# Fetching v behind a tile's second value products, identity products in the opening, and new ranks in a planned attention and feed-forward kernel

## The chip, the cores and the metric

The kernel runs on one core of a Trainium2 chip. The metric is the device time of the whole program in microseconds. Before the change it was 361.08 us, the median of three runs that went from 360.38 to 366.06. The engines are called as the profile calls them: PE is TensorE (PEld its weight loads), DVE is VectorE, ACT is ScalarE, POOL is GpSimd and SP is SyncE, which only issues transfers here.

## The reference

The program is an attention with a window of 32 positions and 8 global positions, followed by a feed-forward layer with softplus.

```python
batch, n_heads, seq, head_dim = (8, 8, 576, 64)
...
scores = scale * np.matmul(q, k.transpose(0, 1, 3, 2))
mask = np.abs(pos[:, None] - pos[None, :]) <= window
mask = mask | is_global[:, None] | is_global[None, :]
scores = np.where(mask, scores, -1000000000.0)
attn = softmax(scores)
x = np.matmul(attn, v)                    # to (8 * 576, 512)
h = x @ w_in                              # 512 -> 2048
g = np.maximum(h, 0.0) + np.log1p(np.exp(-np.abs(h)))
out = g @ w_out                           # 2048 -> 512
```

The softmax is written as one call here. Inputs and output are float32; the kernel computes products in bfloat16.

## The kernel before

**Units and tiles.** The 4608 tokens are cut into 72 units of 64 (9 to a batch). Four units make a quarter tile `n4` (18 of them), and two of these a tile `m` of 512 tokens (9 tiles, numbered 0 to 8 here). A batch boundary falls inside a tile as a rule.

**Preparing a batch.** `load_main` and `load_rest` (L260, L264) fetch k and q into `nq`; TensorE transposes them (`tk`, L614; in batch 0 `tk` L592 and `tq` L603), and the copies go to `kx` and `qx`. `pick` (L537, L548) takes the global rows out, `turn` (L559, tile `gt`) transposes them. `sg` (L677) makes the scores of the global rows, `ov` (L720) their output, which ends in `oz`.

**A unit.** `sc` (L770) makes the scores `s`; `top` (L776, DVE) adds the mask and finds the largest; `ex` (L809, ACT) makes the exponentials `pe`; `su` (L817 to L819, DVE) the sums and `rs`; `no` (L825, POOL) the normalised `pn`, and `gc` (L829, POOL) the columns of the global keys. `pn` is transposed to `pt`. For the first 16 units, and some at the end, TensorE does it (`tp`, L835) and ACT or DVE copies the result. For the others SP issues a DMA transpose (L847).

**Value products.** `val` makes the output `xo` of four units: products with `oz` (L893) and with v in `vA` and `vB` (L906). It needs `pt` of its four units. `xev` copies `xo` to `xT`. `vA` holds a batch's v in 128-row blocks, `vB` the same shifted by 64 rows: SP copies it from `vA` (`shift`, L514 and L515). Both have two buffers, so batch b's v is written over batch b-2's. Five fetches on POOL's queue bring it (`load_v`, L275).

**The feed-forward layer.** `first` (L949) makes `h` in 16 chunks of four matmuls, `soft` (L955, ACT) the softplus `g`; `second` (L960) makes `o` in 4 groups of 16 matmuls, `oev` copies it to `osb`, and SP writes that out (L967). In tile 0 the 512 columns of `h` are cut in two halves. The order of a stage is so: during a tile's `o`, the units of the next tile go through `ex` to `pt`; both its `val` follow, the second one at the very end, and then the next tile's `h` begins.

**The planner.** None of this is in the order in which it is written. Every piece of work is a job with an engine (or two to choose from), a cost, a rank and dependencies. `_Order.run` (L87) takes, again and again, the job that can start soonest by its own costs, the lowest rank first among equals. It gives out PSUM banks by kind (`KINDS`: how many a kind may hold, how many are left spare) and doubles TensorE's costs until some time after the job marked `warms`. The program is then emitted in that order, engine by engine, and each engine works its list in order. The ranks are given at each `o.add` and corrected by three tables: `OPENING`, `LATER` and `OWN`.

Two more things set the fetch of v. The loads of batch b wait for `val` of the quarter tiles that hold units of batch b-2 (L1138), and the loads of k and q of batch b+1 wait for the last fetch of v of batch b (L1086).

```python
    for b in range(2, B):
        held = [T["val", n4] for n4 in range(NU) if any((n4 * 4 + u) // NJ == b - 2 for u in range(4))]
        for job in T["load", b, 2]:
            job["deps"] += [*held, T["ov", b - 2], T["shift", b - 2]]
```

## Time and profile before

| what | value |
|---|---|
| median of three runs | 361.08 us |
| the profiled execution | 360.17 us |
| its span, first to last instruction | 358.3 us |
| mean granted TensorE clock | 0.990 |
| PE, DVE, ACT, POOL busy | 332.8, 224.9, 265.6, 158.4 us |
| first matmul | 6.57 us |
| h of tile 0 begins | 31.01 us |
| h of tiles 1 to 4 begins | 75.15, 115.95, 153.38, 189.68 us |
| transposes by DMA (48), median from issue to landing | 3.6 us |
| fetches of v (40), 96 or 128 KB each, median to landing | 6.4 and 6.8 us |

A busy time is the time in which an engine had an instruction in hand. A row of the view in order of time merges neighbours of one kind: it gives the start of the first, the time until the end of the last, the count, and in brackets the idle time of the engine before it with what ended that. A matmul's end is modelled and reaches some 0.17 us past the start of the next one, so distances are best taken from start to start. "SPq" is the issue of a transfer on SP's queue, not the transfer.

### The profile page before, as it was taken

Reading aid. Unit: us, or ns where it says so; the run is one execution under the profiler, and the core shown is the slowest. Engines: PE = TensorE matmul, PEld = TensorE weight load, DVE = VectorE, ACT = ScalarE, POOL = GpSimd, SP = SyncE. Lnnn points to the kernel's source line nnn. Section 1 sums busy time; section 2 is a strip of 40 time slices with the busy share of each in tenths; the row PEclk is TensorE's granted clock in tenths of the full one; section 3 lists DMA queues with packets and bytes.
Section 4 is the critical chain, followed back from the end, with each engine's and each line's share of the span. In section 5 each row is a group of like instructions: output and inputs, shape, how many; then the busy total and the mean of one; then the engine's idle time right before and its main releaser. Section 6 shows DMA issues by size and latency. Waiting matters only on the chain.

```text
span 358.3 us, 11513 instructions
## 1 busy us (share of the span) xinstructions
PE 332.8 (93%) x4382; PEld 176.5 (49%) x4434; DVE 224.9 (63%) x1044; ACT 265.6 (74%) x738; POOL 158.4 (44%) x268
## 2 busy tenths in 40 slices
PE   1989989999996999999989999999899999999996
PEld 1546775554454444554445445544454454454444
DVE  5886468977696566966796468666865783072011
ACT  3699669985895659885987698859875986774610
POOL 7989732880097204950495047604830370060000
PEclk9999999999997899999999999999999999999999
DMA  6999996099259922997399827993992222021002
GB/s 93 144 235 198 201 133 126 31 153 221 52 129 119 195 44 77 146 159 135 83 132 159 143 82 119 152 166 88 119 118 60 63 82 55 0 75 60 1 29 88
DMA packets 94007, 40.01 MB, mean 112 GB/s; under 512 B 76800, under 2 KB 87424, under 8 KB 93952
## 3 DMA queue, kind: packets, MB, share of 16 engines
q0 software_dynamic: 57056, 18.36, 57.7%
q1 hardware_dynamic: 36896, 20.92, 25.2%
q8 instruction: 34, 0.56, 0.7%
q14 instruction: 21, 0.17, 0.2%
HBM read 36.71 MB, written 9.44 MB: 129 GB/s over the span
## 4 chain that ended last, share of the span: by engine, by line
PE 70%; DMA 8%; DVE 8%; ACT 6%; issue 4%; POOL 3%; SPq 0%; POOLq 0%; DVEq 0%; ACTq 0%
PE h L949 36%; PE o L960 20%; DMA pt<-pn 7%; DVE sm L817 3%; PE s L770 3%; PE xo L906 2%; ACT pe L809 2%; POOL pn L825 2%; DMA kn<-in_k_dram 2%; PE tk L614 1%; PE tp L835 1%; DVE rs L819 1%; ACT L690 1%; ACT pg L690 1%; DVE osb L491 1%
## 5 line engine op out<-in xcount | busy, mean ns | idle before, releaser
L825 POOL TENSOR_TENSOR pn<-pe,rs 128x512 bf16<-128x512 f32 x72 | 74.9, 1041 | 152.5 <-DVE rs L819 140.4
L949 PE MATMUL h<-xT,win 128*128 128x512 bf16 (+1 forms) x620 | 132.7, 362 | 1.3 <-issue 0.2
L960 PE MATMUL o<-wout,g 128*128 128x512 bf16 (+1 forms) x560 | 128.0, 373 | 3.3 <-issue 2.5
L955 ACT ACTIVATE g<-h 128x512 bf16<-128x512 f32 (+1 forms) x160 | 85.2, 557 | 44.7 <-PE h L949 44.3
L809 ACT ACTIVATE pe<-st,nb 128x136 f32<-128x136 f32 x288 | 93.0, 403 | 0.9 <-DVE nb L776 0.9
L949 PEld LDWEIGHTS <-win 128*128 128x128 bf16 x640 | 60.7, 99 | 61.0 <-issue 4.8
L776 DVE CUSTOM_DVE_ANT_0 st<-s,mask 128x136 f32<-128x136 f32 x288 | 65.9, 295 | 38.2 <-PE s L770 38.2
L960 PEld LDWEIGHTS <-g 128*128 128x128 bf16 x592 | 55.1, 98 | 57.0
L817 DVE TENSOR_REDUCE sm<-pe 128x4 f32<-128x544 f32 x60 | 42.6, 710 | 10.7 <-ACT pe L809 10.7
L275 POOL DMA_DIRECT2D vA<-in_v_dram x40 | 34.2, 864 | 0.0
L491 DVE COPY osb<-o 128x512 f32<-128x512 f32 (+1 forms) x23 | 15.3, 664 | 27.5 <-PE o L960 27.2
L776 DVE DVE_READ_ACCUMULATOR2_ANT nb<- 128x1 f32 x288 | 24.0, 83 | 0.0
L819 DVE TENSOR_TENSOR rs<-rs,notg 128x4 f32<-128x4 f32 x72 | 17.9, 249 | 2.5
L491 DVE CAST xT<-xo 128x512 bf16<-128x512 f32 x20 | 13.6, 686 | 7.6 <-PE xo L906 7.5
L491 ACT COPY kx<-tk 128x32 bf16<-128x32 bf16 (+2 forms) x85 | 17.5, 310 | 0.9 <-PE tq L614 0.5
L491 ACT CAST xT<-xo 128x512 bf16<-128x512 f32 x16 | 9.4, 586 | 11.6 <-PE xo L906 11.5
L829 POOL TENSOR_TENSOR gw<-pe,rs 128x32 bf16<-128x32 f32 x72 | 17.2, 240 | 1.0 <-ACT R L491 0.5
L818 DVE RECIPROCAL rs<-sm 128x4 f32<-128x4 f32 x72 | 12.8, 177 | 7.7 <-ACT pe L809 1.5
L770 PE MATMUL s<-kx,qx 64*64 64x136 bf16 x576 | 15.3, 235 | 1.9 <-PE h L949 1.0
L491 DVE COPY qx<-tq 128x512 bf16<-128x512 bf16 (+3 forms) x43 | 16.3, 430 | 1.0 <-PE tq L614 0.7
L906 PE MATMUL xo<-pt,vB 128*64 128x64 bf16 x256 | 12.9, 203 | 3.9 <-DMA pt<-pn 3.9
L770 PEld LDWEIGHTS <-qx 64*64 64x64 bf16 x576 | 10.0, 111 | 12.6 <-issue 12.3
(125 smaller groups left out, 327.1 us busy)
## 6 DMA issues: line engine op xcount, KB each, us to landing
out_dram<-osb SPq DMA_DIRECT2D x35, 256.0 KB, 2.2
vB<-vA SPq DMA_DIRECT2D x16, 256.0 KB, 7.3
nq<-in_k_dram POOLq DMA_DIRECT2D x7, 512.0 KB, 8.1
nq<-in_q_dram POOLq DMA_DIRECT2D x7, 512.0 KB, 12.4
vA<-in_v_dram POOLq DMA_DIRECT2D x24, 128.0 KB, 6.8
win<-in_moe_w_in_dram POOLq DMA_DIRECT2D x2, 1024.0 KB, 15.3
wout<-in_moe_w_out_dram POOLq DMA_DIRECT2D x4, 512.0 KB, 9.1
vA<-in_v_dram POOLq DMA_DIRECT2D x16, 96.0 KB, 6.4
```

Source lines behind the costliest of these rows:

```text
L275: nc.gpsimd.dma_start(out=vA[b % 2][p0:p0 + hi - lo, t, :].rearrange("p (h d) -> p h d", h=H), in_=SRC[2][b, :, lo:hi, :].rearrange("h s d ...
L491: (nc.scalar.copy if e == "ACT" else nc.vector.tensor_copy)(out, in_)
L770: nc.tensor.matmul(out=ps[c, at, :], lhsT=qx[i][r, x * 2 + y, ju * G:(ju + 1) * G], rhs=kf[r, x * 2 + y, ju * W:ju * W + EXT], start=True, ...
L776: nc.vector.tensor_tensor_reduce(out=PS["st", n][:, p, :], in0=s_[:, at, :], in1=mask[:, j, :], scale=-SCALE, scalar=3.0e38, op0=OP.add, o ...
L809: nc.scalar.activation(out=pe[:, p, 0:EXT], in_=PS["st", n][:, p, :], func=AF.Exp, bias=PS["nb", n][:, p:p + 1], scale=-1.0, **({"accum_ou ...
L817: nc.vector.reduce_sum(out=sm[:], in_=PS["pe", n][:, :, 0:EXT], axis=AX)
L819: nc.vector.tensor_tensor(out=rs[:], in0=rs[:], in1=notg[:, j:j + 1].to_broadcast([P, HP]), op=OP.mult)
L825: nc.gpsimd.tensor_tensor(out=pn[:].rearrange("c p (a s) -> c p a s", a=2), in0=wide[:, :, :, 0:G], in1=rs[:].unsqueeze(2).unsqueeze(3).to ...
L906: nc.tensor.matmul(out=PS["xo", n4, half][r, y, x, :], lhsT=vw[:, p * P + c * G:p * P + (c + 1) * G], rhs=PS["pt", n4 * 4 + x][:, p, (c ^ ...
L949: nc.tensor.matmul(out=h[:, :], lhsT=w_in_t[c * P // WC][:, kd, c * P % WC:c * P % WC + P], rhs=PS["xT", m][:, kd, lo:hi], start=(kd == 0) ...
L955: nc.scalar.activation(out=PS["g", m, c][:, lo:hi], in_=PS[key][:, c % 2] if hi - lo <= 256 else PS[key][:, :], func=AF.Softplus)
L960: nc.tensor.matmul(out=PS[key][:, :], lhsT=PS["g", m, kf][:, ns * P:(ns + 1) * P], rhs=w_out_t[kf // 4][:, kf % 4, lo:hi], start=(kf == 0) ...
```

## The change

Five edits, in the planner's inputs alone.

1. The planner reckons a transfer that SP issues as landed 1500 ns after its bytes instead of 1000.
2. A new kind of job: 100 pairs of 128x128 matmuls of the identity with itself, in a chain, rank 50, cost 112 ns a pair, into one PSUM bank that they hold until the last of them. Nothing reads the result. Rank 50 lets them stand only where the planner has no other job for PE. The mark `warms` goes from the first value products to the first of them.
3. PSUM kinds: `s`, `gt`, `tg`, `rt` and `xo` may hold other numbers of banks.
4. The fetch of v of batch b waits for one more `val`: `held[-1] | 1` is the second quarter tile of the tile in which batch b-2 ends. It is a new one for b = 2, 3, 4 and 5 (`val` 3, 5, 7 and 9); for b = 6 and 7 the last one was odd already.
5. The three rank tables are new. Where they move jobs is decided by the planner.

```diff
-                j["at"], j["end"] = t, dma[mine] + 1000
+                j["at"], j["end"] = t, dma[mine] + (1000 if mine == "POOL" else 1500)
...
+    BUSY = 100
...
-    KINDS = dict(h=(4, 0), o=(4, 0), s=(5, 1), pick=(4, 0), gt=(1, 1), tk=(2, 0), tq=(2, 1), tk0=(4, 0), tq0=(3, 0),
-                 sg=(3, 0), tg=(1, 1), ov=(1, 1), tp=(4, 0), rt=(3, 1), xo=(4, 0))
+    KINDS = dict(h=(4, 0), o=(4, 0), s=(4, 0), pick=(4, 0), gt=(3, 0), tk=(2, 0), tq=(2, 1), tk0=(4, 0), tq0=(3, 0),
+                 sg=(3, 0), tg=(1, 0), busy=(1, 0), ov=(1, 1), tp=(4, 0), rt=(4, 2), xo=(3, 2))
...
+    def keep_busy(e, i):
+        if i == 0:
+            PS["busy"] = psum("busy", [P, 2, P], FP32)
+        for x in range(2):
+            nc.tensor.matmul(out=PS["busy"][:, x, :], lhsT=ident_b[:], rhs=ident_b[:], start=True, stop=True)
+
+    last = None
+    for i in range(BUSY):
+        last = T["busy", i] = o.add({"PE": (112, 220)}, lambda e, i=i: keep_busy(e, i), [last], rank=50,
+                                    opens=[("busy", "busy")] if i == 0 else [], uses=["busy"])
...
-    T["val", 0]["warms"] = True
+    T["busy", 0]["warms"] = True
...
-        held = [T["val", n4] for n4 in range(NU) if any((n4 * 4 + u) // NJ == b - 2 for u in range(4))]
+        held = [n4 for n4 in range(NU) if any((n4 * 4 + u) // NJ == b - 2 for u in range(4))]
+        held = [T["val", n4] for n4 in held + [held[-1] | 1]]
...
-    OPENING = dict(blank_l=2.5, gc=-5.5, oev=4.5, ones_l=0.5, su=3.5, top=2.5)
-    LATER = dict(first=1, gev=-1, mx=2, pick=4, qev=2, re=4, sg=1, turn=1.5)
+    OPENING = dict(blank_g=2, blank_l=2.5, first=0.5, gc=-5.5, no=-2.5, oev=2.5, ones_first=0.5, sec=6.5, select=1,
+        su=3.5, top=2.5)
+    LATER = dict(blank_w=-4, fill=-0.5, first=1, gev=-0.5, kev=1.5, mx=2, oz=4, pick=4, re=3, sg=1, su=2.5, turn=1.5,
+        val=2)
```

`OWN`, the table of single jobs, goes from 13 entries to 25 in the same way.

In the emitted order this gives PE 14 identity products before the first transpose of k, 8 before the second half of k, 10 after the first `pick`, 4 and 6 around the last `tq` before the first scores, then 6, 6, 16, 12 and 2 up to `sg`, 114 between `sg` and the first `val`, the longest run of them 28, and 2 behind that `val`. In tile 2 the second `val` stands ahead of both `turn`, where one stood ahead of it before. The fetches of v of batches 2 to 5 stand on POOL's queue behind all the tile's `no`; before, some of these stood between them. In the opening ACT copies five `pt` in place of two and no longer copies `lge` and `R`, which go to DVE. On SP, in tile 2 and later, one output write stands behind a transpose that it preceded.

More of the change, by code (lines that the diff above doesn't have):

```diff
@@ L1137 @@
     for b in range(2, B):
-        held = [T["val", n4] for n4 in range(NU) if any((n4 * 4 + u) // NJ == b - 2 for u in range(4))]
+        held = [n4 for n4 in range(NU) if any((n4 * 4 + u) // NJ == b - 2 for u in range(4))]
+        held = [T["val", n4] for n4 in held + [held[-1] | 1]]
         for job in T["load", b, 2]:
             job["deps"] += [*held, T["ov", b - 2], T["shift", b - 2]]
-    OPENING = dict(blank_l=2.5, gc=-5.5, oev=4.5, ones_l=0.5, su=3.5, top=2.5)
-    LATER = dict(first=1, gev=-1, mx=2, pick=4, qev=2, re=4, sg=1, turn=1.5)
-    OWN = {'make_pos': -2, ('pick', 1, 1): -6, ('qev', 1, 2): -10, ('qev', 1, 3): -10, ('sc', 6, 0): -2, ('sc', 8, 0):
-        -2, ('su', 0): -1, ('tk', 1, 1): -6, ('tk', 1, 3): -6, ('top', 2, 0): -1, ('top', 2, 1): -1, ('turn', 1, 0):
-        -6, ('turn', 1, 1): -6}
+    OPENING = dict(blank_g=2, blank_l=2.5, first=0.5, gc=-5.5, no=-2.5, oev=2.5, ones_first=0.5, sec=6.5, select=1,
+        su=3.5, top=2.5)
+    LATER = dict(blank_w=-4, fill=-0.5, first=1, gev=-0.5, kev=1.5, mx=2, oz=4, pick=4, re=3, sg=1, su=2.5, turn=1.5,
+        val=2)
+    OWN = {'make_pos': -2, ('ex', 6): -1, ('first', 0, 3): 2, ('first', 1, 0): -2, ('first', 1, 1): -2, ('first', 1,
+        4): -4, ('firsth', 0, 5): 4, ('gc', 2): 4, ('kev', 1, 0): -7, ('kev', 1, 1): -7, ('no', 12): 4, ('pick', 1,
+        1): -6, ('re', 2): -1, ('sc', 6, 0): -2, ('sec', 0, 1, 6, 0): 4, ('sec', 0, 2, 12, 0): 4, ('su', 0): -1,
+        ('su', 13): -4, ('su', 4): -4, ('tk', 1, 1): -6, ('top', 16, 1): 4, ('top', 2, 0): -1, ('top', 2, 1): -1,
+        ('top', 3, 1): -4, ('turn', 1, 0): -6}
     BOUND = dict(first=0, soft=0, second=0, oev=0, val=1, rt=1, re=1, xev=1, glob=1, sc=8, top=8, ex=8, su=8, no=8, gc=8, tp=8, pt=8)
```

## Prediction

> **What bounds the kernel now.** I read the page first, then TensorE's rows in order of time, then the stretches around the two places that the change touches.

> ```profile
> span 358.3 us, 11513 instructions
> PE 332.8 (93%) x4382; PEld 176.5 (49%) x4434; DVE 224.9 (63%) x1044; ACT 265.6 (74%) x738; POOL 158.4 (44%) x268
> ...
> PEclk9999999999997899999999999999999999999999
> ```

> TensorE is busy for 93% of the span, so only two things are left to take: its 25 us without work and the time in which its work runs slowly. Of the idle time 6.57 us lie before the first matmul. The clock row shows one dip, near 110 us. It does not show the second slow place, the opening, where the same tiles take twice as long as a little later. The columns of the rows in order of time are start, duration, engine, line, operation, tiles, count and, in brackets, the idle time before.

> ```profile
> 20.12 0.61 PE L835 MATMUL tp<-ident_b,pn 128*128 128x128 bf16 x4
> ...
> 31.01 2.04 PE L949 MATMUL h<-xT,win 128*128 128x256 bf16 x8
> ...
> 35.31 0.39 PE L835 MATMUL tp<-ident_b,pn 128*128 128x128 bf16 x4
> 35.53 1.04 PE L949 MATMUL h<-xT,win 128*128 128x256 bf16 x8
> ```

> Four tp go from 0.61 to 0.39 us and eight h from 2.04 to 1.04. Start to start, an h takes 0.213 us until 33.8 and 0.109 from 33.9 on. So TensorE runs at half speed for the whole opening, although its rows leave it idle for under 5 us between 6.57 and 33.

> The second place is the end of each tile's o products, where the value products (xo, L893 and L906) of the next tile's second half have to come before its first h:

> ```profile
> 108.40 0.59 PE L960 MATMUL o<-wout,g 128*128 128x512 bf16 x2 [0.16 <-issue]
> ...
> 110.91 0.25 PE L559 MATMUL gt<-sel,gk 128*128 128x8 bf16 x4 [1.31 <-DVE gk L491]
> ...
> 113.81 0.26 PE L906 MATMUL xo<-pt,vB 128*64 128x64 bf16 x2 [2.08 <-DMA pt<-pn]
> ...
> 115.95 0.61 PE L949 MATMUL h<-xT,win 128*128 128x512 bf16 x1
> ```
> ```profile
> 220.13 1.89 PE L960 MATMUL o<-wout,g 128*128 128x512 bf16 x8 [0.16 <-issue]
> ...
> 224.75 2.53 PE L949 MATMUL h<-xT,win 128*128 128x512 bf16 x10
> ```

> From the end of o to the first h, tile 2 takes 115.95 - 108.99 = 6.96 us and tile 5 takes 224.75 - 222.02 = 2.73. The same rows give 2.90 in tile 3, 3.48 in tile 4 and 3.66 in tile 6. In tile 2 TensorE waits 2.08 us for a transpose on SP's queue. SP's and GpSimd's rows say why:

> ```profile
> 101.06 3.86 SPq L847 DMA_TRANSPOSE pt<-pn  x3
> ...
> 105.65 5.28 SPq L847 DMA_TRANSPOSE pt<-pn  x3
> ...
> 107.44 1.71 POOL L275 DMA_DIRECT2D vA<-in_v_dram  x2
> ```

> Three transposes take 3.86 us when they run alone and 5.28 with two fetches of v beside them. Unit 23's, issued at 108.40, lands 5.36 us later in the chain of waits; those issued near 101 land 2.5 us after issue. During that wait the clock falls:

> ```profile
> 112.00:113.00 1.00, 0.00 (x0) 0.69 1.95 121
> 113.00:119.00 6.00, 4.97 (x109) 0.50 2.35 150
> 119.00:120.00 1.00, 1.00 (x6) 0.90 1.31 201
> ```

> The third number after the window's own is the granted clock: half speed from 112.4 to 119.2.

> **v behind the tile's second value products.** Four fetches move (batches 2 to 5, beside tiles 1 to 4); those of batches 6 and 7 already waited for a tile's second part. In tile 1 the fetch blocks nothing now. In tile 2 three things go: both gaps, since unit 23's transpose has only other transposes beside it and the new order puts the second value products ahead of the gt that waited 1.31 us, and the dip. Against tile 5's turnaround that is 6.96 - 2.73 = 4.23 us. The slow clock also stretches the h after it: tile 2's h run from 115.95 to the next o at 133.61, 17.66 us; tile 3's from 153.38 to 169.33, 15.95. That is 1.71 more. Tile 3 can gain 2.90 - 2.73 = 0.17 and tile 4 0.75. Upper end: 6.9 us. What is late next is the chain of sum (DVE L817), product (POOL L825) and transpose itself. Tile 6, whose fetch does not move, still waits 0.97 us for it and needs 3.66. If all three became like tile 6, tile 2 would give 3.30 + 1.71, tile 3 lose 0.76 and tile 4 lose 0.18: lower end 4.1. I take 6.5, near the upper end, because tile 3 is already at 2.90.

> What the wait holds up on GpSimd: five v issues (some 0.86 us each) and the four nq issues behind them (0.7 each), which come some 5 us later. The products pn of units 25 and 26, which stood between them, now go ahead. nq was issued from 116.26 to 118.4 and, at the page's median of 12.4 us to landing, was there by 131; its first reader is tile 3's transpose at 147.6. So 16 us of cover stand against 5 us of delay: price 0. The copies of v on SP move from 119.8 to some 125, and SP's next job is at 136.8: price 0. If either cover were gone, it would cost at most the 5 us of delay, once per tile.

> **Identity products.** 200 matmuls of 128 columns enter the opening: 14 before the first transpose of k, 70 more before sg (L677), 114 between sg and the first value products, and 2 right after these. Nothing reads them. Their price is bounded by tp: 0.107 us each at half speed, 0.056 at full (start to start, tp at 32.84 and at 35.31). The first 14 hide in the 6.57 us before k lands.

> What they save for certain, if the clock follows: twelve h (0.104 each) and four tp (0.05 each) between 31.01 and 33.86 run at full speed, 1.45 us. What they do before that has two ends. If the clock is up by about 10 us, TensorE's own 11 us of work before sg halve and pay for the products; ScalarE then loses the 1.26 us it waited for gt at 18.57: a gain of 1.3. If the clock stays low until sg, 70 x 0.107 = 7.5 us, less the gaps of 0.74 and 0.63 us that they fill, stand in front of sg: 6.1 us lost. The windows of before bracket the rise. 13.4 to 16.8 is full of small tiles and leaves the clock low; 31.01 to 33.86 is mostly h, and it rises; after the dip it rises 3.2 us after the first h at 115.95. A block of 14 products at half speed is 1.5 us, the later blocks of 16, 12 and 28 are 1.7, 1.3 and 3.0. So it should be up by the 28 at the latest and probably earlier. I take a gain of 0.4, a third of the good end, because the bad end stays open.

> [...]

> **Ranks.** They move jobs between engines. In the opening ScalarE evicts five pt where it evicted two (3 x 0.49 us start to start) and loses lge and R to VectorE (0.36 + 0.47); it has no gap between 18.97 and 33.4, so this costs 0.65. In later tiles a transpose passes an output write on SP (0.53 us), whose 256 KB nobody waits for: 0, within 1.5 us either way over the kernel, about the spread 2.73 to 3.66 of a turnaround.

> **The sum.** The profiled execution took 360.17 us, 1.87 more than its span. 6.5 + 1.45 + 0.4 - 0.65 = 7.7 less gives 352.5. It lay 0.91 below the median of 361.08, so the forecast is 353.4.

> **The rivals.**
> The products cost in the opening what they gain. The clock comes up only with the block of 28. Then sg is up to 6.1 us later, the late h still gain 1.45, and 6.5 comes from v: 361.08 - 6.5 - 1.45 + 0.65 + 2 to 6 gives 356 to 360. For it speak ScalarE's full row after 19 us, which absorbs nothing; against it that some 40% of each early window is now full-array work.
> [...]
> More comes. k's transposes, the picks and the first scores all halve, the opening gains its full 2.7 and the turnarounds the full 6.9: about 350.
> Slower: the clock takes no notice of identity products. Then 200 x 0.107 = 21.3 us enter an engine that has 2.5 us idle before k and 4.8 after it. Some 14 us are left in front of the first h; v gives back 6.5: about 369. This decides from the point where the clock is still low after the block of 28. Against it: they are plain 128x128 matmuls like h, which did raise it.
> The change does not do what it says: v's order is fixed by a wait on the later product, so that part cannot fail to happen.

> **How the numbers follow.** Forecast 0.50, with 350 to 357 as its own range (4.1 to 6.9 from v, 0.4 to 2.7 from the opening, ranks). Second case 0.21, dip 0.09, more 0.12, slower 0.08. Two per cent of 361.08 is 7.2 us, about what a measurement of this kernel can tell from no change; the bound lies at 353.9, inside the forecast's range. Of its 0.50 I put 0.37 below; with 0.12 from "more" that is 0.49 faster. 0.13 + 0.21 + 0.09 = 0.43 within; 0.08 slower. The range 349 to 361.5 leaves out the slower case and the tails.

> **What would show it.** Right: four tp before 25 us in about 0.39; turnaround of tile 2 near 2.8 and no clock below 1 between 100 and 130; fetches of v starting after the second xo. Wrong: sg (L677 before) later than 19.1, tp still 0.61 after 25, a wait of xo for pt in tile 2, or a new wait of tk or pick for nq.

## The result, and the profile after

The changed kernel takes 364.31 us, the median of 20 executions (360.91 to 368.69), against 360.99 for the kernel before, also the median of 20. The ratio is 1.0114, with a 95% interval of 1.008 to 1.0147: slower by about one per cent. The profiled execution took 363.38 us, with a span of 361.7. One thing is needed to read all numbers here: executions of one kernel differ in whether the clock of TensorE dips, and of 59 executions of the kernel before that ran beside the experiments, the ten with a mean granted clock of 0.998 or more have a median of 356.8 us, the 17 near 0.994 one of 360.4, and the 32 at 0.991 or less one of 361.8.

From the page of the changed kernel come its span, TensorE's busy time, the clock row and the group of the identity products (its tile is called `b`):

```profile
span 361.7 us, 11961 instructions
...
PE 348.5 (96%) x4634; PEld 188.7 (52%) x4634; DVE 219.6 (61%) x1053; ACT 268.0 (74%) x729; POOL 158.6 (44%) x268
...
PEclk9999999999999999999999999999999999999999
...
L1035 PE MATMUL b<-ident_b 128*128 128x128 bf16 x200 | 20.9, 271 | 4.0 <-DVE ident_b L291 4.0
```

This execution has no dip near 110 us, and TensorE's time without work, the span less its busy time, fell from 25.5 to 13.2 us. Its busy time rose by 15.7 us, though, which is more than the 12.3 us of idle time that went. The page's busy time doesn't tell useful work from the 20.9 us of products that nothing reads.

TensorE's rows in order of time show where they lie (start, duration, engine, line, operation, tiles, count, idle time before):

```profile
20.79 1.87 PE L1035 MATMUL b<-ident_b 128*128 128x128 bf16 x16
...
23.13 1.46 PE L1035 MATMUL b<-ident_b 128*128 128x128 bf16 x12
...
25.40 0.73 PE L678 MATMUL sg<-kx,qg 128*32 128x384 bf16 x8
...
27.37 2.96 PE L1035 MATMUL b<-ident_b 128*128 128x128 bf16 x28
...
33.15 1.18 PE L1035 MATMUL b<-ident_b 128*128 128x128 bf16 x18
...
40.65 0.38 PE L950 MATMUL h<-xT,win 128*128 128x256 bf16 x2 [0.69 <-DVE xT L492]
```

Sixteen products in 1.87 us and twelve in 1.46 are half speed; eighteen in 1.18 are full speed. The trace's first record of the full clock is at 29.94, inside the block of 28 (33.86 in the kernel before). sg starts at 25.40 instead of 19.09 and the first h at 40.65 instead of 31.01: 9.64 us later. The first h of the following tiles show how that goes on:

| first h of tile | 0 | 1 | 2 | 3 | 4 | 5 | 6 | end |
|---|---|---|---|---|---|---|---|---|
| before | 31.01 | 75.15 | 115.95 | 153.38 | 189.68 | 224.75 | 261.34 | 358.3 |
| changed | 40.65 | 82.20 | 121.62 | 157.95 | 193.75 | 228.54 | 264.47 | 361.7 |
| later by | 9.64 | 7.05 | 5.67 | 4.57 | 4.07 | 3.79 | 3.13 | 3.4 |

2.6 us come back in tile 0, whose h now all run at full speed, and 3.7 us after tile 1's first h, where the fetch of v was meant to bring 6.5. The turnaround of tile 2, from the end of o to the first h, is 4.71 us, down from 6.96 but not near 2.73:

```profile
119.92 0.22 PE L907 MATMUL xo<-pt,vB 128*64 128x64 bf16 x2 [1.84 <-DMA pt<-pn]
...
121.62 0.59 PE L950 MATMUL h<-xT,win 128*128 128x512 bf16 x2
```

The products still wait 1.84 us there for a transpose on SP. GpSimd's row shows that the fetch of v begins at 117.28, directly behind the tile's last `gw`:

```profile
117.10 0.24 POOL L830 TENSOR_TENSOR gw<-pe,rs 128x32 bf16<-128x32 f32 x1
117.28 4.25 POOL L276 DMA_DIRECT2D vA<-in_v_dram  x5
```

That is after the transpose awaited had been issued (115.57), but 2.64 us before the second value products go on with its result. So the edit puts the fetch behind all `pn` in GpSimd's list, and not behind the second value products: the dependency that it adds is one of the planner, and the profile shows no wait of GpSimd there. In tiles 3, 4 and 5 the fetch begins 0.3 to 0.4 us ahead of the second `val` too. Two questions follow: what the products cost and why the clock took no notice of them for so long, and what else delays those transposes.

### The profile page after: what moved, and what is told of

It is laid out like the page before. It is cut to its first block, busy times and chain, and to the rows that moved or that the text cites. A ratio compares the mean times of both kernels' runs of the same rounds, so it can differ in the third digit from the quotient of the medians.

```text
span 361.7 us, 11961 instructions
## 1 busy us (share of the span) xinstructions
PE 348.5 (96%) x4634; PEld 188.7 (52%) x4634; DVE 219.6 (61%) x1053; ACT 268.0 (74%) x729; POOL 158.6 (44%) x268
## 3 DMA queue, kind: packets, MB, share of 16 engines
q1 hardware_dynamic: 36896, 20.92, 25.5%
## 4 chain that ended last, share of the span: by engine, by line
PE 80%; ACT 7%; DMA 5%; DVE 4%; issue 2%; POOL 1%; DVEq 0%; POOLq 0%; ACTq 0%
PE h L950 35%; PE o L961 25%; ACT pe L810 5%; PE b L1035 4%; DMA pt<-pn 4%; PE s L771 3%; PE xo L907 2%; PE tp L836 2%; PE tk L615 2%; DMA kn<-in_k_dram 1%; PE tq L604 1%; DVE sm L818 1%; PE xo L894 1%; PE sg L678 1%; POOL pn L826 1%
## 5 line engine op out<-in xcount | busy, mean ns | idle before, releaser
L961 PE MATMUL o<-wout,g 128*128 128x512 bf16 (+1 forms) x592 | 132.7, 374 | 0.0
L950 PEld LDWEIGHTS <-win 128*128 128x128 bf16 x640 | 59.7, 98 | 60.1 <-issue 3.6
L276 POOL DMA_DIRECT2D vA<-in_v_dram x40 | 33.9, 867 | 0.0
L492 DVE COPY osb<-o 128x512 f32<-128x512 f32 (+1 forms) x16 | 10.5, 654 | 27.7 <-PE o L961 27.7
L1035 PE MATMUL b<-ident_b 128*128 128x128 bf16 x200 | 20.9, 271 | 4.0 <-DVE ident_b L291 4.0
L1035 PEld LDWEIGHTS <-ident_b 128*128 128x128 bf16 x200 | 16.2, 123 | 6.6 <-DVE ident_b L291 4.0
L492 ACT COPY qx<-tq 128x512 bf16<-128x512 bf16 (+3 forms) x33 | 11.9, 408 | 10.1 <-PE tq L604 7.8
L492 DVE COPY qx<-tq 128x512 bf16<-128x512 bf16 (+3 forms) x31 | 12.4, 437 | 10.6 <-PE tq L615 7.4
L492 ACT COPY kx<-tk 128x32 bf16<-128x32 bf16 (+2 forms) x73 | 15.7, 331 | 0.0
L492 DVE CAST xT<-xo 128x512 bf16<-128x512 f32 x18 | 12.3, 685 | 5.6 <-PE xo L907 5.4
```

Of the source, the lines that this page charges most:

```text
L276: nc.gpsimd.dma_start(out=vA[b % 2][p0:p0 + hi - lo, t, :].rearrange("p (h d) -> p h d", h=H), in_=SRC[2][b, :, lo:hi, :].rearrange("h s d ...
L492: (nc.scalar.copy if e == "ACT" else nc.vector.tensor_copy)(out, in_)
L950: nc.tensor.matmul(out=h[:, :], lhsT=w_in_t[c * P // WC][:, kd, c * P % WC:c * P % WC + P], rhs=PS["xT", m][:, kd, lo:hi], start=(kd == 0) ...
L961: nc.tensor.matmul(out=PS[key][:, :], lhsT=PS["g", m, kf][:, ns * P:(ns + 1) * P], rhs=w_out_t[kf // 4][:, kf % 4, lo:hi], start=(kf == 0) ...
L1035: nc.tensor.matmul(out=PS["busy"][:, x, :], lhsT=ident_b[:], rhs=ident_b[:], start=True, stop=True)
```

## The experiments

**The parts one by one.** First the changed kernel with everything in its place but no product issued:

```
-        for x in range(2):
+        for x in range(0):
             nc.tensor.matmul(out=PS["busy"][:, x, :], lhsT=ident_b[:], rhs=ident_b[:], start=True, stop=True)
```

> The changed kernel with every job in its place, but no identity product is issued (nothing of the output depends on them). Theory (the products, at half speed in front of sg and of the first value products, cost more than they bring): sg near 19.5 instead of 25.4, the clock rises with the first h as before, the first h some 6 to 8 us earlier than 40.65, and the whole about 356 to 358. Rival (the new ranks and the order cost it): first h stays later than 37 and the whole above 361.

354.55 us (353.3 to 356.55); ratio to the kernel before 0.9862 (0.9809 to 0.9916). That is below the 356 to 358 expected: the products alone turn a gain of 1.4% into a loss of 1.1%. The rows that answer to those above:

```profile
19.02 0.73 PE L678 MATMUL sg<-kx,qg 128*32 128x384 bf16 x8
...
31.95 1.39 PE L950 MATMUL h<-xT,win 128*128 128x256 bf16 x5
```

sg is back at 19 and the first h 8.70 us earlier. The clock rises at 34.08, with the h, as in the kernel before.

Then the fetch of v alone, in the kernel before:

```
-        held = [T["val", n4] for n4 in range(NU) if any((n4 * 4 + u) // NJ == b - 2 for u in range(4))]
+        held = [n4 for n4 in range(NU) if any((n4 * 4 + u) // NJ == b - 2 for u in range(4))]
+        held = [T["val", n4] for n4 in held + [held[-1] | 1]]
```

> The kernel before with the fetch of v behind the tile's second value products, and nothing else. Theory (this edit is worth what the prediction said, 4.1 to 6.9): 354.1 to 356.9 against 361, the dip at 112 gone. Rival (the transposes of tile 2 stay slow without v beside them, as the changed kernel's 1.84 us wait hints, so that only the clock's share and one wait go): 357 to 358.5.

355.41 us, inside the theory's range; ratio 0.9875 (0.9823 to 0.9927), some 4.5 us. The dip is gone in the profiled execution, tile 2's turnaround is 3.69 us, tiles 3 and 4 give 0.32 and 1.02, and tiles 5 and 6 take back 1.06 and 0.37. Its span is 4.7 us shorter.

And the changed kernel with the fetch of v where it was (the same lines the other way round):

> The changed kernel with the fetch of v where it was. If the two parts add up, it is as much slower than the changed kernel as the other one-part kernel is faster than the kernel before: 364 + 3 to 5 = 367 to 369. Rival (the new ranks and the later start had moved the dip anyway): 364 to 365.

364.58 us, 0.3 above the changed kernel, ratio 1.0107 (1.0042 to 1.0172): the rival. The parts don't add up. So the new order was run with neither of the other two parts. What is left of the change there is the new ranks, the PSUM kinds and the 1500 ns, planned with the products in their places, though none is issued:

> The new ranks alone: no product is issued and v is fetched where it was in the kernel before. If the v edit is worth its 5 us in this order too: 354.5 + 5 = 359 to 360.5. Rival (the new ranks had already taken the dip and the wait in tile 2 away, as the changed kernel with the old fetch of v, 0.3 us slower than the changed one, hints): 354 to 356.

355.79 us, ratio 0.9893 (0.9845 to 0.994): again the rival. No execution of it shows a dip (granted clock 0.999 to 1.0 in all six). By the ratios the new order and the v edit together bring 1.4%, where they bring 1.1% and 1.25% alone. GpSimd's rows in tile 2 of this kernel say why:

```profile
109.43 1.04 POOL L826 TENSOR_TENSOR pn<-pe,rs 128x512 bf16<-128x512 f32 x1
110.43 0.24 POOL L830 TENSOR_TENSOR gw<-pe,rs 128x32 bf16<-128x32 f32 x1
110.61 4.26 POOL L276 DMA_DIRECT2D vA<-in_v_dram  x5
```

The new order by itself already puts all five fetches of batch 3 behind the tile's last `pn`, where the v edit puts them, and its turnaround of tile 2 is 2.97 us with the v edit and without it. In tiles 3 and 4 the fetches still stand between the `pn`, and the turnarounds are 2.46 and 2.65 us, against 2.46 and 2.72 with the v edit. So the two parts take away the same loss, that of tile 2, by the same means.

**Which products cost.** The first 84 alone, up to sg, and the last 116 alone, after it:

```
+        for x in range(2 if i < 42 else 0):      # the other kernel: i >= 42
```

> The changed order with only the first 84 identity products (14 ahead of k, 70 between k and sg); the 116 after sg are not issued. Theory (at half speed each product in front of sg moves sg by its own 0.107 us, less the gaps it fills): sg near 25.4 as in the changed kernel, first h about 3 to 4 us earlier than 40.65, clock up only with the h, whole 354.5 + 6 = 360 to 361. Rival (the products before sg are mostly absorbed and those after it cost): sg below 22, whole below 358.

> The changed order with only the 116 products after sg. Theory: sg at 19.0 as without products, the clock comes up in the first window that is mostly products, one window (3.4 us) or two before the first h, the products cost 3 to 5 us in front of the first h and give back about 1.5 by the late h: whole 354.5 + 2 to 4 = 356.5 to 358.5. Rival (these bring the clock up early enough to pay): 354 or less.

With the first 84: 364.36 us, ratio 1.0139 (1.008 to 1.0198), all of the loss and more than the theory gave; sg at 25.46, first h at 37.90, and turnarounds of 5.66 and 3.50 us in tiles 2 and 3 on top. With the last 116: 356.31 us, ratio 0.9898 (0.9835 to 0.996), just under the theory's range and 1.8 above none, with overlapping intervals; sg at 19.19, first h at 35.09, 3.1 later, of which 2.6 are left at tile 1. The clock came up at 25.08 there, inside a dense stretch:

```profile
21.16 3.19 PE L1035 MATMUL b<-ident_b 128*128 128x128 bf16 x28
...
24.57 0.86 PE L1035 MATMUL b<-ident_b 128*128 128x128 bf16 x8
```

So the clock does take notice of identity products: here it came up behind a block of 28 that took 3.19 us and in the eight after it. Raising it 9 us earlier than the h did was still not worth 116 products: the first h comes 3.1 us later for them.

**A block at the front.** Would the clock pay if it were up from the start? 56 products of a tile of ones, ahead of all else on TensorE, in the kernel of the v edit alone:

```
+    nc.vector.memset(full_b[:], 1.0)
...
+        for x in range(56):
+            nc.tensor.matmul(out=ps[:, x % 4, :], lhsT=full_b[:], rhs=full_b[:], start=True, stop=True)
```

> The v edit alone, and 56 products of a tile of ones, in one block, ahead of everything on TensorE (from about 0.5 us; nothing reads them, and they end near 6.5 at half speed). Theory (what raises the clock is one of its windows of 3.4 us that is nearly full of full-array products): the clock is up before 8 us, and the small tiles of the opening then run at twice the speed if the clock stays up; first h near 27 to 29 and the whole 350 to 353. Rival 1 (it is raised, but falls again in the first window of small tiles, as at 112 in the kernel before): the clock shows one short high stretch, whole within 1 us of the v edit alone. Rival 2 (products that nothing reads do not raise it): k's transposes up to 0.9 us later, whole up to 1 us slower than the v edit alone.

356.41 us, 1.0 above the v edit alone, with overlapping intervals; ratio 0.9911 (0.9874 to 0.9948): the first rival. The clock rose at 6.15, with the block, and fell at 12.98, among the small tiles. Windows of that kernel (from:to, length, PE busy and count, granted clock, share of the DMA engines, GB/s), cut where its clock records lie, and four of TensorE's rows:

```profile
2.74:6.15 3.41, 3.41 (x35) 1.00 0.80 111
6.15:9.57 3.42, 2.50 (x83) 1.00 1.06 149
9.57:12.98 3.41, 2.44 (x96) 1.00 1.09 117
12.98:16.39 3.41, 2.14 (x48) 0.50 2.21 166
```
```profile
1.15 5.67 PE L1036 MATMUL b<-full_b 128*128 128x128 bf16 x56 [1.15 <-DVE full_b L256]
6.75 0.71 PE L595 MATMUL tk<-ident_b,kn 72*64 72x72 bf16 x32
...
14.45 1.04 PE L551 MATMUL pick<-qn,pick 40*32 40x512 bf16 x8 [1.27 <-DMA qn<-in_q_dram]
...
18.16 0.73 PE L680 MATMUL sg<-kx,qg 128*32 128x384 bf16 x8
```

(Ahead of the first record the clock column says 1.00 whatever the clock is; the spacing of the products tells.) k's transposes take 0.71 us where they took 1.17. Yet sg starts at 18.16, and at 18.10 without the block. The faster matmuls wait for transfers: 0.92 us for k, 0.44 for the first part of q and 1.27 for the second, which lands between 14.2 and 15.0 us in all the profiled kernels. From 14.45 on the work up to sg takes 3.7 us at half speed, with the block and without it. So a faster TensorE had nothing to gain ahead of 14.4 us. What it would gain between there and sg no run shows, because the clock was low there in all of them.

Then a block and single products behind it, to keep the clock up, in the changed order:

```
-        for x in range(2):
+        for x in range(56 if i == 0 else i > 6):
```

> The changed order with 56 products of a tile of ones ahead of everything, none of the next 14, and one product instead of two at each later place (93). Theory (a block raises the clock at about 6 us and a product here and there keeps it up): no fall before the first h, sg at 19 to 20, first h before 31, whole 352 to 355. Rival 1 (it falls again as after the block alone): 93 products at half speed, some 5 us in front of the first h, whole 357 to 360. Rival 2 (it stays up but the opening up to sg waits for ScalarE and VectorE, and what the products cost is not paid back): sg at 18.5 to 20, whole 355 to 357.

359.94 us, ratio 1.0011 (0.9967 to 1.0055): rival 1. In the profiled execution, at 356.27 the fastest of the twelve, the clock fell at 13.54 and came back at 27.20; sg starts at 21.09 and the first h at 35.01. In the window before the fall TensorE was busy for 71% of the time, 14 points of which were products.

**The waits of tiles 2 and 3.** Without products, in the same order, tile 2 took 2.97 us and tile 3 2.46; with 84 products 5.66 and 3.50, with all 200 4.71 and 3.42. GpSimd's work before these waits has the same spacing without products and with all 200, so a later start alone should not matter. The trace also lists transfers on a queue that the page calls instruction. From part 3 of two pages (queue and kind, packets, MB, share), without products and then with 84 very small ones (below):

```profile
q8 instruction: 34, 0.56, 0.6%
```
```profile
q8 instruction: 35, 0.57, 0.7%
```

Each is 16 KB and occupies a DMA engine for some 0.9 to 1.8 us. The pages count 4434, 4518 and 4634 weight loads on TensorE without products, with 84 and with 200. With one matmul to each load its lists have some 8870, 9040 and 9270 instructions, an estimate from these counts, and there are 34, 35 and 36 such packets: one for some 258 to 261 instructions by these counts. From the first packet to the last, the traces of the kernel before and of the changed one hold 249 and 252 records of TensorE's instructions to a packet. The estimate from these four counts is one fetch for some 255 instructions; 256 is what is tried below. If what counts is beside which transposes these fetches fall, then the length of the list matters, and by its remainder to that number alone. This can be tried at little cost in the opening: 200, 84 or 128 very small products ahead of k, where TensorE is idle (200 of them took 5.50 us), and none later.

```
+        for x in range(200 if i == 0 else 0):      # and 84, and 128
+            nc.tensor.matmul(out=PS["busy"][0:32, x % 2, 0:8], lhsT=full_b[:, 0:32], rhs=full_b[:, 0:8], start=True, stop=True)
```

> The changed order; in place of the 200 products stand 200 very small ones (32 columns of weights, 8 of data), all ahead of k's transposes, where TensorE is idle for 6 us (some 0.03 us each, so they end near 6.5). TensorE's list is then as long as the changed kernel's, 400 instructions more than without products, at no cost in the opening. Theory (what TensorE's turnaround in tiles 2 and 3 loses beside the opening comes from where the fetches of its instructions, 16 KB each, fall beside the transposes on SP): sg near 19.2 and first h near 32 as without products, but turnarounds as in the changed kernel, tile 2 near 4.7 and tile 3 near 3.4. Rival (the later start of everything lengthens them): tile 2 near 3.0, tile 3 near 2.5 as without products.

> The same with 84 very small products: the list is as long as in the kernel with the products up to sg alone. Theory (place of the fetches): tile 2 near 5 or more and tile 3 near 3.5, as there (5.66 with a dip of the clock, 3.50). Rival (later start): tile 2 near 3.0, tile 3 near 2.5.

> The changed order with 128 very small products ahead of k instead of the 200 products: TensorE's list is 256 instructions longer than without products, one fetch of 16 KB more, so that every later fetch falls beside the same instructions again. Theory (place of the fetches): turnarounds as without products, tile 2 near 3.0 and tile 3 near 2.5, whole 354 to 355.5. Rival (a longer list, or the very small products as such, lengthen them): tile 2 above 4.5 and tile 3 above 3.4 as with 84 and with 200, whole 357 to 362.

| products in front | list longer by | sg | first h | turnaround, tile 2 | tile 3 | span |
|---|---|---|---|---|---|---|
| none | 0 | 19.02 | 31.95 | 2.97 | 2.46 | 351.7 |
| 84 | 168 | 19.35 | 32.24 | 5.69 | 4.34 | 356.0 |
| 128 | 256 | 19.89 | 32.78 | 2.98 | 2.46 | 351.4 |
| 200 | 400 | 21.06 | 34.01 | 5.86 | 4.55 | 360.4 |

The kernel with 128 has a median of 355.18 us and a ratio of 0.9888 (0.9792 to 0.9984), as without products; single executions of the other two took 357.7 and 362.08. Both lists that by this estimate shift the fetches lose time in the two turnarounds, 4.6 and 5.0 us, each with a dip of the clock in tile 2, and the one that is longer by one fetch loses nothing. Two kernels from above fit: with the last 116 products the list is 232 longer, 24 short of one fetch, and the turnarounds are 2.97 and 3.40; with the block and 93 products it is 298 longer, 42 past one fetch, and they are 2.98 and 2.46. One detail missed: with 200 the opening loses 2 us too, where TensorE stops for 2.11 us within k's transposes with nothing in the profile that it waits for.

SP's rows of tile 2 show the transposes themselves, without products, with 84 and with 128:

```profile
99.87 3.86 SPq L848 DMA_TRANSPOSE pt<-pn  x3
```
```profile
100.86 5.40 SPq L850 DMA_TRANSPOSE pt<-pn  x3
```
```profile
100.77 3.85 SPq L850 DMA_TRANSPOSE pt<-pn  x3
```

The second has a 16 KB fetch at 101.5 that took 1.75 us, inside its first transpose. Everything on SP behind it comes 1.5 us later. The two transposes that TensorE needs last land at 111.17 and 112.57, beside a second fetch at 108.9 and the fetch of v, issued from 109.70 on; without products the same two land at 108.51 and 108.99, and v is issued from 108.71 on. So TensorE waits:

```profile
111.22 0.22 PE L909 MATMUL xo<-pt,vA 128*64 128x64 bf16 x2 [0.88 <-DMA pt<-pn]
...
112.61 0.27 PE L909 MATMUL xo<-pt,vB 128*64 128x64 bf16 x2 [1.18 <-DMA pt<-pn]
```

In the view of the tile pt, who waited for it (us, times), in the kernel with 84 and in that with 128:

```profile
  PE xo L909: 4.1, 4
```
```profile
  PE xo L909: 1.0, 2
```

**Planned without products.** The order without products was planned with them. Planning with none:

```
-    BUSY = 100
+    BUSY = 0
-    T["busy", 0]["warms"] = True
+    T["val", 0]["warms"] = True
```

> The new ranks and the v edit, planned without any product (the clock taken as warm from the first value products, as in the kernel before). Theory (the order that was planned around the products costs nothing once they are gone): 354 to 356, as the changed order without products (354.55). Rival (planned without them the opening is shorter, since nothing was put behind a product): first h below 31 and 352 to 353.5.

359.93 us, ratio 1.0019 (0.9982 to 1.0055): both missed. The opening is worse (first h at 34.37, TensorE idle for 2.16 us before a tp that waits for a sum on VectorE), and the turnarounds of tiles 1 and 2 are 6.23 and 4.51. The tables of ranks fit one order, and another order starts anew.

## Why the prediction was wrong

The forecast was 7.7 us less than the profiled execution before; it became 3.2 more.

**The step that failed is the price of the identity products before sg**: "I take a gain of 0.4, a third of the good end, because the bad end stays open." The bad end, 6.1 us, is what came: sg 6.3 us later. Two things in it were wrong. The clock "should be up by the 28 at the latest and probably earlier": it was the latest; the two windows before held 53% and 60% of products and did not raise it, although TensorE was never idle in them. And the good end, in which "TensorE's own 11 us of work before sg halve and pay for the products", left out that the second half of q lands at some 14.4 us. With the clock up from 6.15 to 12.98 sg did not come earlier (18.16 against 18.10). Only the last 3.7 us ahead of sg could have halved. How much of that sg would keep is open, but it is at most 1.9 us, an estimate from these 3.7, against the 6 us.

**The 114 products between sg and the first value products were named, and neither the sum nor the second case has a price for them.** In the changed kernel the way from sg to the first h is 15.25 us, and 12.93 without products; the last 116 alone cost 3.1 at the first h. The second case, the first of the rivals, had the clock right, up with the block of 28, and its 356 to 360 was too low for the same omission: with 2.3 more for these, and 3.7 instead of 6.5 for what came after tile 1's first h, it comes to 361 to 365.

**v behind the second value products, 6.5 us (4.1 to 6.9), was right in size for that edit alone**: some 4.5 by the ratio, 4.7 in the spans. Tile 2's gap gave 3.26 instead of 4.23, its stage lost the dip as forecast, and tiles 5 and 6 gave 1.4 back. In the changed kernel only 3.7 came after tile 1's first h. The step had two readings wrong. "v's order is fixed by a wait on the later product" is not so: the fetch follows the last `pn` and runs beside the transpose awaited. And the 5.28 us of the three transposes were not due to v alone: the first of them, at 105.65, took 2.65 us where the three ahead of it took 1.22 or 1.23, with a 16 KB fetch of instructions at 106.25 inside it, and v was first issued at 107.44. So the step missed that transposes were also slow beside the fetches of TensorE's own instructions, and that 400 more instructions moved those fetches: tile 2 at 4.71 and tile 3 at 3.42 instead of 2.97 and 2.46. That nq has cover held: nothing waited for it.

**The late h, 1.45**, came: tile 0 gave back 2.6, this and more. **The ranks, 0.65 lost**: with the v edit the new order starts the first h 1.5 us later and ends 2.0 earlier in the spans, 0.9 in the medians, whose intervals overlap. What was not foreseen is that the new order by itself already moves the fetch of batch 3 and so takes the dip away.

Of the four signs named for a wrong prediction three came: sg late, tp slow after 25 us (0.63 at 26.94) and the wait of xo for pt in tile 2. The wait for nq did not. Of the signs for a right one only the clock's came, full between 100 and 130 us.

## What to carry to other kernels

Work put into gaps to raise a clock has to be priced at the low clock (0.107 us a product here, against 0.056 at the full one), every instruction of it, up to the place where the trace shows that the clock rises, and its gain counts only where TensorE, and not a transfer or a copy on another engine, sets the pace. Ask first what the stage would gain from a faster engine: here, up to the landing of q at 14.4 us, the answer was nothing. A dependency given to a planner need not be a wait in the program: see in the trace where the transfer really starts. The best kernel of this study is the changed one with the products left out (354.55 us), and the one with a list 256 instructions longer is as good; the v edit alone (355.41) and the new order alone (355.79) cannot be told from it, their intervals overlap. This kernel waits for transposes by DMA, and in it even instructions that cost next to nothing themselves moved the time by one per cent (spans of 351.7 and 356.0 us with none and with 84).

## What the runs showed of the hardware

**Fetches of instructions beside DMA transposes.** Over the 14 profiled kernels the landing is known for 586 transposes of pt. Those with neither v nor a transfer of the two queues called instruction in flight, from 1.2 us after their issue until their landing, landed after a median of 2.43 us (199 of them). Without v and with one such transfer it was 3.29 (92), with two 4.30 (22). Longer transposes meet more fetches, so the count alone proves no cause; the lists of different length show it, in tiles 2 and 3 (tile 2: 2.97 and 2.98 us with none and 128, 5.69 and 5.86 with 84 and 200).
